# First feed-forward layer: the output unit three iterations behind its h tile, and the rests' pass last over all four chunks

## The chip, the cores and the metric

One Trainium2 chip, one core. The metric is device time in microseconds (us) of one execution of the whole program, as the median of several runs. A core has five engines with a queue each: TensorE (PE; its weight loads are shown apart as PEld), VectorE (DVE), ScalarE (ACT), GpSimd (POOL), and SyncE (SP), which here only issues DMAs. PE writes into PSUM, eight banks of 128 partitions by 2 KiB; DVE and ACT read PSUM and SBUF, POOL SBUF alone.

## The reference

Three parts in a row, in fp32:

```python
# attention over a packed set of 32 queries, 8 batches, 8 heads, 576 tokens, head size 64
p_packed = sm_attn(p, k, v)
x = sm_attn(q, p_packed, p_packed)      # then laid out as 4608 tokens x 512
# first layer: 512 -> 2048 -> 512
h = x @ w_in
g = np.maximum(h, 0.0) + alpha * np.minimum(h, 0.0)
x = g @ w_out
# second layer: 512 -> 1536 -> 512
g = x @ w_gate
x = (g / (1 + exp(-g)) * (x @ w_val)) @ w_out
```

The weights of both layers arrive as fp64 words, which the kernel turns into fp32 on the chip.

## The kernel before

An fp32 product is made of three passes of a faster matmul type (fp32r). Each operand is split into a rounded part (`hi`) and the rest (`lo`), and `mm3` (L284) adds up lo weights x hi data, hi weights x hi data, and hi weights x lo data (the rests' pass). In the profile these passes are lines L287, L288 and L289.

**The first layer** is one loop of 256 iterations (`N1`), each for one half batch `j` (288 tokens) and one slice `f` of 128 of the 2048 inner features; `order` (L648) gives the pairs. For the first two batches the slices come in two halves, so that there are 8 partial sums of 8 iterations each, and then 12 sums of 16. Iteration `it` has up to two units on PE:

- `h_unit(it)` (L734): 6 matmuls of 128x288 into one of two PSUM banks tagged `h`. The attention's second product is folded into the weights (`ppw`, made by `pp_win`, L574), so the data are the attention's weights `a2`. Then g: for the first 48 iterations (`RELU`) two Relus on ACT (L753 into the single buffer `r`, L754 into `g32`) and one DVE instruction (L755); from then on two DVE instructions that read the bank (L759, L762). `g32` has two buffers.
- `split` (L767): ACT casts `g32` to `hi` (L770), POOL subtracts to get `lo` (L772). Each has `LAG1 + 1` = 3 buffers.
- `o_unit(it - LAG1)` (L775), two iterations behind: for each of four chunks `dc` of 128 output features, the three passes into the bank `acc0` to `acc3` of that chunk, 12 matmuls in all. At the end of a sum (`stop`) the four banks are copied out, by ACT (L798) and DVE (L796) in turn, or all four added by DVE to the first half's sum (L794, for the four second halves), and stored with two DMAs on SP (L799) to `x1p` or `x1d`. `load_part` reads `x1p` back, `load_x` reads `x1d` for the second layer.

**Around these units** a table of steps (`plan`, `EARLY`, `PPW`, `STEPS`) puts the attention of later batches, the `pp_win` products, and the conversion of weights (`widen`, L205: one ACT instruction, some five on DVE, one or two on POOL for each piece of 512 columns) at given iterations, ahead of the h unit or between it and the output unit. From iteration 44 on the weights of the second layer are converted, combined (`product2`, L686) and written to DRAM (`wgvd`).

**What sets the order.** Within an engine the order is not the source's word for word. The kernel is laid out by a planner (`schedule_with_timeline_sim=True`, L1072) that takes each engine's instructions by readiness, as it reckons it, and by the source's order where several are ready; it adds the waits. On the chip each engine then runs its fixed order. What the change touches: `LAG1` (L21), the call of `split` at L765, `split` itself, `o_unit`, and by `LAG1` the main loop (L1026 to L1032).

Of the kernel before, what the change touches and what calls it, by code (L numbers as in the profile page):

```python
# [9 lines left out]
F32R = mybir.dt.float32r  # L10
# [7 lines left out]
P = 128  # L18
T = 384
WP = 4  # L20
LAG1 = 2  # L21
RELU = 48


# [72 lines left out]
def f32(ap):  # L97
    return ap.bitcast(F32)
# [3 lines left out]
def tile_kernel(  # L102
# [21 lines left out]
    nc = tc.nc  # L124
# [3 lines left out]
    KC = DM // P  # L128
# [31 lines left out]
    def utile(tag, shape, name, dt=F32):  # L160
        return upool.tile(shape, dt, tag=tag, name=name, bufs=UBUFS[tag])
# [122 lines left out]
    def mm3(o, wts, xs, start, stop, **kw):  # L284
        whi, wlo = wts
        xhi, xlo = xs
        nc.tensor.matmul(o, wlo, xhi, start=start, stop=False, **kw)  # L287
        nc.tensor.matmul(o, whi, xhi, start=False, stop=False, **kw)  # L288
        return nc.tensor.matmul(o, whi, xlo, start=False, stop=stop, **kw)  # L289
# [303 lines left out]
    for f in range(NF1):  # L593
# [10 lines left out]
        c=quad(2, natural=True),  # L604
# [120 lines left out]
    gp = gp1.enter_context(tc.tile_pool(name="g1", bufs=1))  # L725
    gs, acc, part = {}, {}, {}
# [7 lines left out]
    def h_unit(it):  # L734
        j, f, _, _ = order[it]
        b, half = divmod(j, 2)
        w = ppw[b, f // WP]
        c = slice((f % WP) * P, (f % WP + 1) * P)
        tok = slice(half * HS, (half + 1) * HS)
        hp = ps.tile([P, 512], F32, tag="h", name=f"h{it}", bufs=2)[:, :HS]  # L740
        for q2 in range(NQ):
            hi, lo = a2[NQ * b + q2]
            mm3(
                hp,
                (w[:, q2, c], w[:, NQ + q2, c]),
                (hi[:, tok], lo[:, tok]),
                q2 == 0,
                q2 == NQ - 1,
            )
        g32 = gp.tile([P, HS], F32, tag="g32", name=f"g32_{it}", bufs=2)  # L750
        if it < RELU:
            r = gp.tile([P, HS], F32, tag="r", name=f"r_{it}")
            begun[it] = nc.scalar.activation(out=r, in_=hp, func=AF.Relu)  # L753
            nc.scalar.activation(out=g32, in_=hp, func=AF.Relu, scale=-1.0)  # L754
            nc.vector.scalar_tensor_tensor(  # L755
                out=g32, in0=g32, scalar=nal[:, f : f + 1], in1=r, op0=ALU.mult, op1=ALU.add
            )
        else:
            nc.vector.tensor_scalar(  # L759
                out=g32, in0=hp, scalar1=0.0, scalar2=al[:, f : f + 1], op0=ALU.min, op1=ALU.mult  # L760
            )
            nc.vector.scalar_tensor_tensor(  # L762
                out=g32, in0=hp, scalar=0.0, in1=g32, op0=ALU.max, op1=ALU.add
            )
        gs[it] = split(gp, g32, it, LAG1 + 1)  # L765

    def split(pool, x, n, bufs):  # L767

        hi = pool.tile(list(x.shape), F32R, tag="hi", name=f"hi{n}", bufs=bufs)
        nc.scalar.activation(out=hi, in_=x, func=AF.Copy)  # L770
        lo = pool.tile(list(x.shape), F32R, tag="lo", name=f"lo{n}", bufs=bufs)
        nc.gpsimd.tensor_tensor(out=lo, in0=x, in1=f32(hi), op=ALU.subtract)  # L772
        return hi, lo

    def o_unit(it):  # L775
        j, f, start, stop = order[it]
        gx = gs.pop(it)
        hi, lo = wout[f // WP]
        for dc in range(KC):
            if start:  # L780
                acc[dc] = ps.tile([P, 512], F32, tag=f"acc{dc}", name=f"acc{dc}_{it}")[:, :HS]
            c = slice(dc * P, (dc + 1) * P)
            mm3(acc[dc], (hi[:, f % WP, c], lo[:, f % WP, c]), gx, start, stop)
        if not stop:
            return
        if f != NF1 - 1:
            x1p[j] = dram.tile([P, KC, HS], F32, name=f"x1p{j}")
        dst = x1d[j] if f == NF1 - 1 else x1p[j]
        for pr in range(2):
            xs = part[j][pr] if j in part else utile("x", [P, 2, HS], f"x1s{it}_{pr}")  # L790
            for i in range(2):
                a = acc[2 * pr + i]
                if j in part:
                    nc.vector.tensor_tensor(out=xs[:, i, :], in0=a, in1=xs[:, i, :], op=ALU.add)  # L794
                elif i:
                    nc.vector.tensor_copy(out=xs[:, i, :], in_=a)  # L796
                else:
                    nc.scalar.activation(out=xs[:, i, :], in_=a, func=AF.Copy)  # L798
            nc.sync.dma_start(out=dst[:, 2 * pr : 2 * pr + 2, :], in_=xs)  # L799
# [35 lines left out]
    def split_x(s, name):  # L835

        if name == "S2":
            src = raws_of(s, "A11")
            for e in range(2):
                nc.vector.tensor_tensor(  # L840
                    out=src[e], in0=raw2[s, "S1"][e], in1=src[e], op=ALU.subtract
                )
        elif name == "S4":
            src = raws_of(s, "A12")
            for e in range(2):
                nc.vector.tensor_tensor(
                    out=src[e], in0=src[e], in1=raws_of(s, "A11")[e], op=ALU.subtract
                )
        elif name == "S3":
            src = raws_of(s, "A21")  # L850
        else:
            src = raw2[s, "S1"] if name == "S1" else raws_of(s, name)
        tag = X_TAGS[name]
        x = wpool.tile([P, 2, 2, T], F32R, tag=tag, name=f"x{name}_{s}", bufs=WBUFS[tag])
        for e in range(2):
            nc.scalar.activation(out=x[:, 0, e], in_=src[e], func=AF.Copy)
            nc.vector.tensor_tensor(out=x[:, 1, e], in0=src[e], in1=f32(x[:, 0, e]), op=ALU.subtract)
        xs2[s, name] = x
# [22 lines left out]
    for n in ("load", "A11", "S", "S2", "A22", "A12", "S4", "S3", "S1"):  # L881
        fn = dict(load=lambda: load_x(0), S=lambda: sums_x(0)).get(
            n, lambda n=n: split_x(0, n)
# [138 lines left out]
    def steps(it, late):  # L1022
        for s in plan.get((it, late), ()):
            s()

    for it in range(N1 + LAG1):  # L1026
        steps(it, 0)
        if it < N1:
            h_unit(it)
        steps(it, 1)  # L1030
        if it >= LAG1:
            o_unit(it - LAG1)  # L1032
    gp1.close()
# [43 lines left out]
```

## Time and profile before

| | us |
|---|---|
| median of 3 runs | 1752.83 (1747.44 to 1753.05) |
| the profiled execution | 1762.42 |
| its span, first to last instruction | 1760.6 |
| PE busy in the span | 1669.6 (95%) |
| DVE / ACT / POOL busy | 1019.8 / 606.4 / 797.9 |
| first layer's loop in the span | from about 45 to 886 |

The rows are from the profiled execution. A busy time is the union of an engine's instructions; matmuls are pipelined and their ends are modelled, so the distance from one start to the next tells more than a matmul's duration. A row of waits names the engine that waited, its line and what ended the wait. In a row of a group the part after the second bar is the idle time ahead of these instructions and what ended it.

### The profile page before, as it was taken

To read this page: it belongs to the slowest core of one execution; us is meant where nothing else is said; L and a number is where in the kernel's file an instruction comes from. 1 tells how busy PE (TensorE), PEld (TensorE's weight loads), DVE (VectorE), ACT (ScalarE), POOL (GpSimd) and SP (SyncE) were. 2 spreads that over 40 slices of the span, in tenths; PEclk is the share of its full clock that TensorE was granted. 3 is DMA by queue.
4 is the path that set the end of the run, shared out by engine and by line. 5 is a ranking of instruction groups with operands and counts; after the bars stand their busy time and mean duration, and the time that the engine had idled before them with its cause. 6 is when DMAs were issued, how large, how long until landed. Compare 5 with 4: busy or idle time off the path is not lost.

```text
span 1760.6 us, 27334 instructions
## 1 busy us (share of the span) xinstructions
PE 1669.6 (95%) x10048; PEld 1474.1 (84%) x10048; DVE 1019.8 (58%) x1875; ACT 606.4 (34%) x1384; POOL 797.9 (45%) x824
## 2 busy tenths in 40 slices
PE   5698899999999999999999999999999999999997
PEld 3477688888788788889989989988988998998996
DVE  7999878676867768684633353354354344335332
ACT  5765553343433344342222232232132122223121
POOL 3666756555654555533433333334334333333332
PEclk7799999999999999999999999999999999999999
DMA  9333365455445455431364464464355445445342
GB/s 237 120 96 118 117 177 162 132 144 133 120 131 138 124 160 142 127 101 38 127 233 168 153 212 168 147 218 150 147 200 182 150 176 189 166 167 181 149 168 78
DMA packets 227750, 266.04 MB, mean 151 GB/s; under 512 B 130848, under 2 KB 190240, under 8 KB 227616
## 3 DMA queue, kind: packets, MB, share of 16 engines
q1 hardware_dynamic: 227616, 264.30, 46.9%
q8 instruction: 79, 1.29, 0.3%
q14 instruction: 55, 0.45, 0.1%
HBM read 214.70 MB, written 49.55 MB: 150 GB/s over the span
## 4 chain that ended last, share of the span: by engine, by line
PE 63%; DVE 10%; POOL 8%; DMA 7%; issue 7%; ACT 4%; SPq 1%; POOLq 0%; ACTq 0%; DVEq 0%
PE acc L287 5%; PE acc L289 5%; PE o L287 5%; PE acc L288 5%; PE o L288 4%; PE o L289 4%; PE yb L289 3%; PE yb L287 3%; PE yb L288 3%; DMA wgvd<-cva 3%; PE h L287 2%; PE xb L287 2%; PE xb L288 2%; PE xb L289 2%; PE vb L288 2%
## 5 line engine op out<-in xcount | busy, mean ns | idle before, releaser
L772 POOL TENSOR_TENSOR lo<-g,hi 128x288 fp32r<-128x288 f32 x256 | 224.0, 877 | 219.8 <-ACT hi L770 181.9
L960 POOL TENSOR_TENSOR s<-s,p 128x384 f32<-128x384 f32 x72 | 75.5, 1048 | 487.6 <-ACT s L959 487.3
L770 ACT ACTIVATE hi<-g 128x288 fp32r<-128x288 f32 x256 | 112.8, 441 | 253.5 <-DVE g L762 175.9
L919 DVE TENSOR_TENSOR u<-vb,u 128x384 f32<-128x384 f32 x144 | 80.2, 557 | 187.2 <-PE vb L289 187.2
L287 PE MATMUL o<-wp,pl 128*128 128x512 f32 x432 | 171.6, 397 | 16.1 <-POOL pl L988 15.7
L289 PE MATMUL o<-wp,ph 128*128 128x512 f32 x432 | 171.9, 398 | 0.0
L288 PE MATMUL o<-wp,ph 128*128 128x512 f32 x432 | 171.6, 397 | 0.0
L287 PE MATMUL h<-a2h,ppw 128*128 128x288 f32 x512 | 159.0, 311 | 7.8 <-DVE ppw L587 4.7
L919 DVE TENSOR_TENSOR u<-yb,p 128x384 f32<-128x384 f32 x144 | 79.6, 553 | 130.5 <-PE yb L289 128.3
L988 POOL TENSOR_TENSOR pl<-s,ph 128x384 fp32r<-128x384 f32 x144 | 142.6, 1011 | 26.0 <-ACT ph L986 21.8
L289 PE MATMUL h<-a2l,ppw 128*128 128x288 f32 x512 | 152.1, 297 | 0.0
L288 PE MATMUL h<-a2h,ppw 128*128 128x288 f32 x512 | 151.8, 297 | 0.0
L759 DVE TENSOR_SCALAR g<-h,al 128x288 f32<-128x288 f32 x208 | 105.7, 508 | 77.1 <-PE h L289 62.3
L959 ACT ACTIVATE s<-p 128x384 f32<-128x384 f32 x72 | 37.8, 525 | 303.1 <-DVE p L919 303.0
L287 PEld LDWEIGHTS h<-a2h,ppw 128*128 128x128 f32 x512 | 96.8, 189 | 39.0 <-DVE g L762 10.4
L986 ACT ACTIVATE ph<-s 128x384 fp32r<-128x384 f32 x144 | 73.3, 523 | 145.8 <-DVE s L964 129.6
L943 DVE TENSOR_TENSOR s<-xb,s 128x384 f32<-128x384 f32 x72 | 40.1, 557 | 134.2 <-ACT s L942 134.2
L287 PEld LDWEIGHTS o<-wp,pl 128*128 128x128 f32 x432 | 81.7, 189 | 30.9 <-POOL pl L988 23.9
L287 PE MATMUL xb<-xA,gv 128*128 128x384 f32 x288 | 97.9, 340 | 6.7 <-DVE u L919 6.3
L289 PEld LDWEIGHTS h<-a2l,ppw 128*128 128x128 f32 x512 | 96.5, 189 | 3.8 <-issue 3.8
L287 PE MATMUL vb<-xS,gv 128*128 128x384 f32 x288 | 97.2, 338 | 1.1 <-DVE u L919 1.1
L288 PEld LDWEIGHTS h<-a2h,ppw 128*128 128x128 f32 x512 | 96.9, 189 | 1.4 <-issue 1.4
(184 smaller groups left out, 4835.2 us busy)
## 6 DMA issues: line engine op xcount, KB each, us to landing
gv<-wgvd SPq DMA_DIRECT2D x144, 896.0 KB, 5.7
wgvd<-cva SPq DMA_DIRECT2D x84, 256.0 KB, 2.6
cva<-in_moe_w_out_dram SPq DMA_DIRECT2D x28, 512.0 KB, 3.6
v<-in_v_dram SPq DMA_DIRECT2D x16, 576.0 KB, 5.7
out_dram<-os SPq DMA_DIRECT2D x12, 768.0 KB, 3.7
cva<-in_moe_w_in_dram SPq DMA_DIRECT2D x16, 512.0 KB, 3.7
kr<-in_k_dram SPq DMA_DIRECT2D x96, 72.0 KB, 2.7
qr<-in_q_dram SPq DMA_DIRECT2D x96, 72.0 KB, 2.4
```

Of the source, the lines that this page charges most:

```text
L287: nc.tensor.matmul(o, wlo, xhi, start=start, stop=False, **kw)
L288: nc.tensor.matmul(o, whi, xhi, start=False, stop=False, **kw)
L289: return nc.tensor.matmul(o, whi, xlo, start=False, stop=stop, **kw)
L759: nc.vector.tensor_scalar(out=g32, in0=hp, scalar1=0.0, scalar2=al[:, f : f + 1], op0=ALU.min, op1=ALU.mult)
L770: nc.scalar.activation(out=hi, in_=x, func=AF.Copy)
L772: nc.gpsimd.tensor_tensor(out=lo, in0=x, in1=f32(hi), op=ALU.subtract)
L919: nc.vector.tensor_tensor(out=out, in0=bank, in1=x, op=ALU.add)
L943: nc.vector.tensor_tensor(out=s1, in0=xb, in1=s1, op=ALU.mult)
L959: nc.scalar.activation(out=s2, in_=p1, func=AF.Sigmoid)
L960: nc.gpsimd.tensor_tensor(out=s2, in0=s2, in1=p1, op=ALU.mult)
L986: nc.scalar.activation(out=hi, in_=x, func=AF.Copy)
L988: nc.gpsimd.tensor_tensor(out=lo, in0=x, in1=f32(hi), op=ALU.subtract)
```

## The change

The output unit of iteration `it` now comes in the loop's iteration `it + 3`. `hi` gets a fourth buffer; `lo` keeps three, through a new argument of `split`. And `o_unit` issues its 12 matmuls in another order: for each chunk the two passes over `hi` data, four chunks in turn, and then the rests' pass for the four chunks. `start` and `stop` stay with the first and the last matmul of each chunk. The loop has one iteration more; the number of instructions on each engine is the same.

```diff
-LAG1 = 2
+LAG1 = 3
...
-        gs[it] = split(gp, g32, it, LAG1 + 1)
-
-    def split(pool, x, n, bufs):
+        gs[it] = split(gp, g32, it, LAG1 + 1, LAG1)
+
+    def split(pool, x, n, bufs, bufs_lo):
...
-        lo = pool.tile(list(x.shape), F32R, tag="lo", name=f"lo{n}", bufs=bufs)
+        lo = pool.tile(list(x.shape), F32R, tag="lo", name=f"lo{n}", bufs=bufs_lo)
...
         hi, lo = wout[f // WP]
+        ghi, glo = gx
         for dc in range(KC):
             if start:
                 acc[dc] = ps.tile([P, 512], F32, tag=f"acc{dc}", name=f"acc{dc}_{it}")[:, :HS]
             c = slice(dc * P, (dc + 1) * P)
-            mm3(acc[dc], (hi[:, f % WP, c], lo[:, f % WP, c]), gx, start, stop)
+            nc.tensor.matmul(acc[dc], lo[:, f % WP, c], ghi, start=start, stop=False)
+            nc.tensor.matmul(acc[dc], hi[:, f % WP, c], ghi, start=False, stop=False)
+        for dc in range(KC):
+            c = slice(dc * P, (dc + 1) * P)
+            nc.tensor.matmul(acc[dc], hi[:, f % WP, c], glo, start=False, stop=stop)
```

## Rows read from the trace of the kernel before

**Rows 1.** The page: busy time of each engine, and DVE in 40 slices.

```profile
PE 1669.6 (95%) x10048; PEld 1474.1 (84%) x10048; DVE 1019.8 (58%) x1875; ACT 606.4 (34%) x1384; POOL 797.9 (45%) x824
...
DVE  7999878676867768684633353354354344335332
```

**Rows 2.** Stretches: length, each engine's busy us (instructions), clock, DMA, GB/s.

```profile
core 0: us, PE busy (x) PEld busy (x) DVE busy (x) ACT busy (x) POOL busy (x), PEclk, DMA share, GB/s
45.00:130.00 85.00, 66.81 (x425) 50.01 (x421) 80.78 (x133) 61.68 (x141) 52.29 (x44) 0.88 0.38 108
130.00:205.00 75.00, 64.79 (x410) 53.10 (x409) 70.30 (x98) 38.51 (x96) 51.75 (x43) 1.00 0.35 112
205.00:400.00 195.00, 192.34 (x1363) 164.87 (x1362) 144.41 (x293) 84.06 (x209) 112.61 (x127) 1.00 0.54 149
400.00:600.00 200.00, 192.47 (x1350) 163.74 (x1350) 145.69 (x289) 77.32 (x187) 108.13 (x123) 1.00 0.49 133
600.00:886.00 286.00, 283.49 (x2062) 256.53 (x2060) 193.98 (x385) 101.21 (x244) 136.94 (x161) 1.00 0.42 120
```

**Rows 3.** Waits of PE in 205 to 890 us: total us, times, longest us.

```profile
PE acc L289 <- POOL lo L772: 1.8, 5, 0.6
PE acc L287 <- ACT hi L770: 1.8, 3, 1.1
PE h L287 <- DVE g L762: 1.4, 3, 0.8
```

**Rows 4.** By line, 205 to 890 us: busy us, mean ns, idle before.

```profile
L772 POOL TENSOR_TENSOR lo<-g,hi 128x288 fp32r<-128x288 f32 x222 | 190.6, 860 | 197.4 <-ACT hi L770 159.4 <-issue 11.7 <-PE acc L289 10.0
...
L759 DVE TENSOR_SCALAR g<-h,al 128x288 f32<-128x288 f32 x208 | 105.7, 508 | 77.1 <-PE h L289 62.3 <-POOL lo L772 12.2 <-POOL cva L694 1.6
L770 ACT ACTIVATE hi<-g 128x288 fp32r<-128x288 f32 x222 | 97.7, 441 | 213.2 <-DVE g L762 175.9 <-DVE g L755 8.9 <-DVE mx L444 5.2
L762 DVE SCALAR_TENSOR_TENSOR g<-h,g 128x288 f32<-128x288 f32 x208 | 93.3, 450 | 3.3
```

**Rows 5.** Waits of PE in 130 to 205 us.

```profile
PE acc L287 <- ACT hi L770: 6.5, 7, 1.6
...
PE acc L287 <- DVE x1s L796: 0.8, 1, 0.8
PE acc L289 <- POOL lo L772: 0.3, 1, 0.3
```

**Rows 6.** Timeline, 139.9 to 142.2 us: start, us, engine, line.

```profile
139.89 1.54 DVE L755 SCALAR_TENSOR_TENSOR g<-g,nal,r 128x288 f32<-128x288 f32 x1
...
141.46 0.44 ACT L770 ACTIVATE hi<-g 128x288 fp32r<-128x288 f32 x1 [2.34 <-DVE g L755]
...
141.96 0.40 PE L287 MATMUL acc<-hi,wo0l 128*128 128x288 f32 x1 [1.62 <-ACT hi L770]
...
142.19 0.29 PE L288 MATMUL acc<-hi,wo0h 128*128 128x288 f32 x1
```

**Rows 7.** Waits of PE in 45 to 130 us.

```profile
PE acc L287 <- ACT hi L770: 1.2, 1, 1.2
```

**Rows 8.** Timeline of PE, 155.3 to 156.2 us.

```profile
155.28 0.29 PE L288 MATMUL acc<-hi,wo1h 128*128 128x288 f32 x1
155.41 0.29 PE L287 MATMUL h<-a2h,ppw 128*128 128x288 f32 x1
155.54 0.69 PE L289 MATMUL acc<-lo,wo1h 128*128 128x288 f32 x4
```

**Rows 9.** Timeline, 709.5 to 711.3 us, at the end of one sum.

```profile
709.52 0.39 ACT L798 ACTIVATE x1s<-acc 128x288 f32<-128x288 f32 x1
...
710.21 0.29 PE L289 MATMUL acc<-lo,wo3h 128*128 128x288 f32 x1
...
710.49 0.81 DVE L796 COPY x1s<-acc 128x288 f32<-128x288 f32 x2
```

**Rows 10.** Tile acc: who waited for it (us, times).

```profile
  POOL lo L772: 10.0, 4
```

## Prediction

> **What bounds the kernel now.** I read four views in order: the page for the whole, a table of stretches to see where TensorE (PE) is short of work, PE's waits in those stretches, and single rows of the timeline. PE is busy for 1669.6 us of the span [rows 1]. The first layer lies between about 45 and 886 us, and it has two regimes [rows 2]. From 45 to 205 us PE is busy for 131.6 of 160 us while VectorE (DVE) is busy for 151.1: DVE is full, with the weight conversions, and PE starves. From 205 to 886 us PE is busy for 668.3 of 681 us at the full granted clock of 1.00, with DVE at 68% to 74%: PE is the bound. An iteration's own matmuls are 6 for h and 12 for the output; in a run they start 0.13 us apart (155.28 to 155.41, and four in 0.69 us) [rows 8], so an output unit is 1.6 us, an h unit 0.8 and an iteration 2.4, of which 256 make 610 us that the change leaves as they are. So only PE's idle time can move, and of that only what ends with the operands of the output unit: 3.6 us in 8 waits after 205 us [rows 3], 6.8 in 8 waits from 130 to 205 [rows 5], and 1.2 before that [rows 7].
>
> **The change part by part.** The profiled execution is 1762.42 us (span 1760.6), 0.55% over the median of 1752.83; I make the sum against it and carry it over by the ratio.
>
> *The lag after 205 us.* Between the end of h(k) and the start of o(k), PE has o(k-2), h(k+1), o(k-1) and h(k+2): 4.8 us of cover. With a lag of three it is 7.2. What must fit beneath it is 0.51 + 0.45 us on DVE, 0.44 on ScalarE (ACT) and 0.86 on GpSimd (POOL), 2.3 us in all [rows 4], plus what those queues hold ahead of it. The 8 waits are the times when 4.8 us was too little, by 1.1 us at the most [rows 3], so 2.4 us more covers each. A matmul after a wait costs another 0.1 us (0.40 us and a next start 0.23 us later [rows 6], against 0.13). That is 3.6 + 0.8 = 4.4 us at most and zero at least. What is late next is h(k+3), which needs the bank of h(k+1); its cover, o(k-2), h(k+2) and o(k-1), stays 4.0 us at either lag, and it already waited 3 times [rows 3]. The waits for the rests, 1.8 us, have nothing to do with that bank, while the waits for `hi`, 1.8 us, come from a late DVE and can return there. I take 1.8 + 0.9 + 0.8 = 3.5 us gained.
>
> *The lag from 45 to 205 us.* Here o(k) waits since DVE has only just made g: DVE ends L755 at 141.43 after 1.54 us, ACT casts at 141.46, PE starts at 141.96 after 1.62 us idle [rows 6]. Putting h(k+3) ahead of o(k) gives PE nothing to do: the bank that it needs is released by the two Relus of h(k+1), the first of which writes `r`, a single buffer that DVE's g(k) has to read first. The wait for `hi` becomes a wait for the bank. DVE's own work is not changed, and it has 4.7 us idle in 75 [rows 2]. Bounds: all waits go, 6.5 + 0.8 + 0.3 and 9 restarts of 0.1, 8.5 us gained [rows 5]; or PE stands one output unit further back at 205 us, 1.6 us lost. I take zero, and zero for the 1.2 us before 130 us.
>
> There is a rule that reads this stretch otherwise. The Trainium skill, Perfetto Trace Analysis, "Optimization Strategy", says that the same gap coming back on the engine that should be saturated can mean too few buffers for the next tile. By that rule the fourth `hi` buffer would earn the 8.5 us; DVE's 70.3 busy of 75 us [rows 2] speaks against it, and it is a rival below.
>
> *The order of passes.* The same 12 matmuls and 12 weight loads per unit. The trace holds the new order already, since the planner holds back rests that are late: after l, h on four chunks come the four rests together, 0.69 us, with starts 0.13 us apart [rows 8], as in any other order. Cost zero.
>
> *The end of a sum.* 20 sums end, 19 with a unit behind them. Now the banks end 0.13 us apart instead of 0.4, so the first bank is done 0.8 us later and the second 0.5 later; the next unit's chunks also begin 0.26 us apart rather than 0.4. In the stop at 710 us the last matmul starts at 710.21 and DVE's two copies run from 710.49 to 711.30 [rows 9]: DVE was busy elsewhere when its first bank ended, so they don't move. ACT's first copy goes from 709.52 to about 710.3, over by 710.7. The next unit starts after an h unit, at 711.14: covered, and the fourth bank, wanted at 711.9, has 0.6 us to spare. Where the cover is gone, the one such wait of 130 to 205 us was 0.8 us [rows 5]: from 0 to 19 x 0.8 = 15 us. The stop read here is covered, so I take one such wait, 1 us lost. The four second-half sums whose four additions all go to DVE are the likeliest.
>
> *The buffers.* `hi` has four now, `lo` stays at three at a lag of three. So POOL's lo(k+3) needs o(k)'s rests to be through, 1.6 us after h(k+3); its operand is ready after 0.51 + 0.45 + 0.44 = 1.4 us, so POOL stands about 0.2 us each time with its other work queued behind. It stood for such a buffer 4 times before, 10.0 us in all [rows 10]. Who waits for it: g(k+5) on DVE, since `g32` has two buffers (DVE stood 12.2 us for `lo` [rows 4]). lo(k+3) ends 0.86 us after o(k); h(k+5) ends 0.8 + 1.6 + 0.8 = 3.2 us after o(k), 2.3 us later. Zero, while POOL begins it within 2.3 us.
>
> *Moved past queues.* Everything that an output unit issues goes one iteration later: its copies on ACT and DVE and its two stores per sum on SP, which pass what SP has due in 2.4 us. The readers of x1p and x1d come iterations later: nothing. The drain after the last h grows from two units to three, the start lacks one: zero. The second layer is untouched.
>
> Sum: -3.5 + 1 = -2.5 us; 1762.42 - 2.5 = 1759.9, a ratio of 0.9986, times 1752.83 gives **1750.3 us**.
>
> **The rivals.** *Starvation is relieved.* The waits from 130 to 205 us go after all, since some of them are only POOL and ACT out of step and DVE has 4.7 us of slack. For it: 8 of the 17 operand waits lie there. Against it: the single `r`. -2.5 - 8.5 = -11, or 1741.8 us.
>
> *The rests' buffers throttle.* POOL, held at lo(k+3), lets its other work pile up, a 2.3 us margin is passed, DVE's g(k+5) is late, and PE waits for a bank of h. Its price is the longest such wait, 0.8 us [rows 3]. With 3.5 us gained it passes the bound of slower from 11 such iterations on; 15 of the 222 after 205 us give 12.0 - 3.5 = +8.5, or 1761.3 us. For it: POOL's 10.0 us and DVE's 12.2 us of such waits [rows 4, 10]. Against it: POOL is 48% to 58% busy [rows 2].
>
> *It does not do what it says.* The planner orders by readiness: in the trace a rests' pass stands between matmuls of an h unit [rows 8], which no line of the source asks for. If the lag only breaks ties, nothing moves: 1752.8 us.
>
> *Cycling through banks breaks the stream.* With a bank changed at 8 places in each unit rather than at 4, PE restarts once in each: 256 x 0.1 = 25.6 us [rows 6], less 2.5, or 1776 us. Against it: the run of four banks at 0.13 us [rows 8] and a clock of 1.00 throughout [rows 2]. The Trainium skill, TensorE: Matmul & The Clock Gate, "A second HAM failure mode: psum-queue depth-cycling", describes it: a kernel whose matmuls go round the banks idles briefly between groups, and its clock swings. Those rows disagree with it here.
>
> **How the numbers follow.** A measurement of this kernel can tell about 0.3%, 5.3 us, from no change. Chances: forecast 0.42, starvation relieved 0.28, throttle 0.18, does nothing 0.08, banks 0.04. The forecast's own range is 1746 to 1756 (0 to 4.4 gained, the end of sums, 1.6 lost); a tenth of it falls below 1747.6. Faster 0.28 + 0.04 = 0.32; same 0.38 + 0.08 = 0.46; slower 0.18 + 0.04 = 0.22. The range has to take in the first rival's 1741.8 and half of the second's: **1741 to 1760**. Left out: the banks and the far half of the throttle, and the far ends of the costs.
>
> **What would show it.** Right: the waits of PE on `hi` and `lo` after 205 us nearly gone, those on the bank of h (g at L762) longer by about 1 us; from 130 to 205 us the same idle time of PE, some 10 us, with DVE as full, ended by other waits; four rests in a row in nearly every unit at 0.13 us. Wrong: PE ahead by 5 us or more at 205 us (starvation); many waits of POOL for the rests' matmuls with waits of h behind them (throttle); an unchanged order on PE (nothing); starts further apart inside units (banks). It would also be wrong if the waits of attention's steps, which the change doesn't touch, were dealt anew by the planner.

## The result, and the profile after

| | kernel before | changed kernel |
|---|---|---|
| median, us | 1749.59 (1745.38 to 1753.05) | 1760.57 (1756.9 to 1762.36) |
| ratio, 95% interval | 1 | **1.0053 [1.0035, 1.0071]** |
| profiled execution, us | 1762.42 (span 1760.6) | 1759.17 (span 1757.4) |

The change makes the kernel slower by 0.53%, about 9 us (the two medians lie 11 us apart; the interval of the ratio, 6 to 12 us, holds both). The forecast was 1750.3 us in 1741 to 1760: wrong in sign, and outside the range.

One thing has to be put aside before the traces are read side by side. The profiled execution of before is longer than that of after, against the verdict. I took a second profile of the unchanged kernel (experiment 1). The tables below cut both profiles of before, and that of after, some 2 to 5 us behind the first matmul of the second layer. The columns are those of [rows 2].

Before, first profile:

```profile
45.00:885.00 840.00, 798.90 (x5593) 687.26 (x5590) 634.39 (x1193) 361.89 (x873) 461.72 (x495) 0.99 0.45 128
885.00:1760.00 875.00, 843.98 (x4317) 771.23 (x4315) 353.56 (x612) 218.23 (x455) 319.47 (x296) 0.99 0.47 169
```

Before, second profile:

```profile
45.00:885.00 840.00, 800.51 (x5597) 689.37 (x5594) 635.54 (x1194) 362.99 (x875) 462.61 (x495) 0.99 0.45 128
885.00:1750.00 865.00, 837.06 (x4313) 768.69 (x4311) 340.91 (x612) 219.19 (x455) 325.04 (x296) 1.00 0.47 171
```

After:

```profile
45.00:891.00 846.00, 800.59 (x5592) 690.50 (x5589) 638.53 (x1195) 360.98 (x873) 463.51 (x495) 0.99 0.45 127
891.00:1757.00 866.00, 838.12 (x4320) 769.46 (x4318) 341.12 (x612) 219.62 (x455) 325.19 (x296) 1.00 0.47 171
```

From the second layer's first matmul to the end the first profile of before took 879.7 us, the second 869.3 and every other run 864 to 873; that excess belongs to that one execution. The first layer is the same in both: the second layer's first matmul starts at 880.9 and 880.4 us. In the changed kernel it starts at 888.9. So **all of the loss, 8 us, is in the first layer**. Cut exactly there, the second profile of before and that of after read:

```profile
45.00:880.40 835.40, 795.91 (x5565) 684.77 (x5562) 635.26 (x1193) 362.37 (x873) 461.81 (x494) 0.99 0.45 127
45.00:888.90 843.90, 798.49 (x5579) 688.40 (x5576) 638.53 (x1195) 360.98 (x873) 463.51 (x495) 0.98 0.45 127
```

Of the 8.5 us between these two, PE stands for 5.9 (45.4 against 39.5 us) and is busy for 2.6 more.

The granted clock of TensorE is a rival that the expectations don't name. In the changed kernel it is 0.50, the lower of its levels of 1.2 and 2.4 GHz, from 196.6 to 200.0 us, behind 10 us in which PE stood for 2.4. Matmuls that started 0.13 us apart then start 0.24 apart, and four rests take 1.16 us where they take 0.69 at the full clock:

```profile
196.99 0.44 PE L784 MATMUL acc<-hi,wo1l 128*128 128x288 f32 x1
197.22 0.44 PE L785 MATMUL acc<-hi,wo1h 128*128 128x288 f32 x1
...
197.94 1.16 PE L788 MATMUL acc<-lo,wo1h 128*128 128x288 f32 x4
```

Neither profile of before has such a stretch between 100 us and the second layer; every other kernel below has at least one. Averaged over whole executions the granted clock is 0.987 for before and 0.984 for the changed kernel; taken as span times the missing share, 6 us more are lost. Yet this explains little of the 9 us. In this profile the stretch lies where DVE is full, and by 205 us PE has done about as many matmuls as before (829 since 45 us, before 835 and 827). And among executions of the same kernel (205, of 18 kernels) 1 us more of lost clock goes with 0.19 us more of time (95%: 0.09 to 0.29): about 1 us of the 9, an estimate. No run holds the clock fixed.

The page of after, as in [rows 1]:

```profile
PE 1665.5 (95%) x10048; PEld 1476.1 (84%) x10048; DVE 1010.9 (58%) x1875; ACT 606.8 (35%) x1384; POOL 805.4 (46%) x824
...
DVE  6999978686777768675543353353354336335332
```

The stretches of after, as in [rows 2]:

```profile
45.00:130.00 85.00, 67.49 (x414) 50.43 (x411) 80.44 (x134) 60.07 (x138) 50.51 (x42) 0.87 0.33 101
130.00:205.00 75.00, 64.21 (x415) 54.79 (x414) 70.29 (x97) 41.01 (x101) 54.92 (x45) 0.98 0.42 121
205.00:400.00 195.00, 183.98 (x1305) 157.01 (x1304) 148.17 (x284) 81.01 (x203) 108.83 (x123) 1.00 0.55 148
400.00:600.00 200.00, 198.57 (x1411) 171.80 (x1409) 150.12 (x300) 77.95 (x193) 116.61 (x134) 1.00 0.50 136
600.00:886.00 286.00, 281.33 (x2021) 251.48 (x2020) 188.69 (x381) 100.48 (x241) 131.84 (x154) 1.00 0.39 111
```

Up to 205 us PE is as busy as it was (131.7 us of 160, before 131.6). From 205 to 400 us it loses 8.4 us (192.34 to 183.98), from 400 to 600 it gains 6.1 back, and from 600 to 886 it loses 2.2. These stretches are cut by time and not by work, so they don't add up to the 8 us; but the loss has no single place, it comes and goes.

PE's waits in after, 205 to 890 us, as in [rows 3] (engine, line, what ended the wait: total us, times, longest us):

```profile
PE h L287 <- DVE g L762: 7.1, 9, 1.9
PE ppt L506 <- ACT ppbd L500: 2.8, 3, 1.3
PE ppt L506 <- DVE x1p L799: 2.1, 1, 2.1
PE et L473 <- ACT E L448: 1.4, 2, 0.7
PE pp L489 <- DVE ppw L587: 1.2, 2, 1.0
PE acc L784 <- DVE x1p L799: 0.9, 1, 0.9
PE pp L489 <- DVE s2t L521: 0.8, 1, 0.8
PE acc L784 <- ACT x1s L803: 0.5, 1, 0.5
```

The waits for `hi` and `lo`, 3.6 us before, are gone. In their place stand 7.1 us for the bank of h, and 4.9 us of attention's `ppt`, 0.6 before, 2.1 of it ended by a copy of a sum; attention's `et` and `pp` wait as long as they did (3.4 us, before 3.5). In sum PE waited 16.8 us here, against 12.0 and 10.4 in the two profiles of before.

PE's waits in after, 130 to 205 us, as in [rows 5]:

```profile
PE h L287 <- ACT g L754: 4.4, 4, 2.1
PE acc L784 <- ACT hi L770: 2.8, 3, 1.4
PE acc L784 <- DVE x1s L801: 2.7, 2, 2.1
```

Two rows by line, 205 to 890 us, as in [rows 4]:

```profile
L772 POOL TENSOR_TENSOR lo<-g,hi 128x288 fp32r<-128x288 f32 x222 | 189.9, 858 | 215.8 <-ACT hi L770 133.8 <-PE acc L788 36.2 <-issue 21.4
...
L759 DVE TENSOR_SCALAR g<-h,al 128x288 f32<-128x288 f32 x208 | 105.1, 507 | 83.4 <-PE h L289 74.3 <-POOL lo L772 8.0 <-POOL cva L694 0.6
```

POOL is held by the rests' matmuls for 36.2 us, before 10.0 (12.2 in the second profile); but DVE waits for `lo` no longer than before: 8.0 us, where the two profiles of before have 12.2 and 6.6.

A unit of after in the timeline, columns as in [rows 6]: the last chunk's two passes over `hi`, the four rests in one row, the next h unit.

```profile
216.65 0.30 PE L784 MATMUL acc<-hi,wo3l 128*128 128x288 f32 x1
216.78 0.29 PE L785 MATMUL acc<-hi,wo3h 128*128 128x288 f32 x1
216.91 0.69 PE L788 MATMUL acc<-lo,wo3h 128*128 128x288 f32 x4
217.44 0.29 PE L287 MATMUL h<-a2h,ppw 128*128 128x288 f32 x1
```

### The profile page after: what moved, and what is told of

The parts are those of the page before. It is cut to its first block, busy times and chain, and to the rows that moved or that the text cites. A ratio compares the mean times of both kernels' runs of the same rounds, so it can differ in the third digit from the quotient of the medians.

```text
span 1757.4 us, 27301 instructions
## 1 busy us (share of the span) xinstructions
PE 1665.5 (95%) x10048; PEld 1476.1 (84%) x10048; DVE 1010.9 (58%) x1875; ACT 606.8 (35%) x1384; POOL 805.4 (46%) x824
## 4 chain that ended last, share of the span: by engine, by line
PE 67%; DVE 12%; DMA 6%; issue 5%; POOL 4%; ACT 4%; SPq 1%; DVEq 0%; ACTq 0%; POOLq 0%
PE o L287 5%; PE o L288 5%; PE o L289 5%; PE acc L784 5%; PE acc L785 5%; PE acc L788 5%; PE yb L287 4%; PE yb L288 4%; PE yb L289 4%; PE xb L287 3%; PE xb L288 3%; PE xb L289 3%; PE h L287 3%; PE vb L288 2%; PE vb L289 2%
## 5 line engine op out<-in xcount | busy, mean ns | idle before, releaser
L971 POOL TENSOR_TENSOR s<-s,u 128x384 f32<-128x384 f32 x72 | 101.2, 1406 | 5.6
```

The lines of the kernel that those rows point to most:

```text
L971: nc.gpsimd.tensor_tensor(out=s2, in0=s2, in1=u3, op=ALU.mult)
```

## The experiments

Four theories stood at the start. *Throttle*: three `lo` buffers at a lag of three hold up POOL. *The lag itself*: with h ahead of the output unit, waits for operands turn into waits for the bank of h. *Ends of sums*: the four banks now end 0.13 us apart, and the copies are late. *Layout*: none of these; the planner orders all engines anew whenever the source changes, and the new order is worse in places that have nothing to do with the change. For each run the start of the second layer ("x") says how much of a difference lies in the first.

### 1. The unchanged kernel once more

> The kernel before, unchanged, for a second profile of it. All theories: ratio 1.000 within 0.002. Its first profile took 1762.4 us where the median is 1751: if the second layer is 869 us long here, as in the five other kernels, and not 880, that profile's excess was its own; if it is 880 again, the order of the second layer differs from the others and the first layer of the kernel before must be some 10 us shorter than its profile showed.

Measured: 0.9996 [0.9981, 1.001], x 880.4. The comparison is good to 0.2% either way, and the tables above show what the first profile had too much.

### 2. Each half of the change alone

The lag with the old order of passes, and the new order with the old lag:

```diff
 # lag alone, against the changed kernel
-            nc.tensor.matmul(acc[dc], lo[:, f % WP, c], ghi, start=start, stop=False)
...
+            mm3(acc[dc], (hi[:, f % WP, c], lo[:, f % WP, c]), gx, start, stop)
```

```diff
 # order alone, against the changed kernel
-LAG1 = 3
+LAG1 = 2
...
-        gs[it] = split(gp, g32, it, LAG1 + 1, LAG1)
+        gs[it] = split(gp, g32, it, LAG1 + 1, LAG1 + 1)
```

> The lag of three with four hi and three lo buffers, but the passes in the order of the kernel before (lo weights, hi weights, rests, chunk by chunk). Throttle by the rests' buffers: as the changed kernel, 9 us over the kernel before (ratio 1.005), and POOL's waits for the rests' matmuls near the 36.2 us in 14 that the changed kernel shows (10.0 in 4 before). The lag itself (h ahead of o turns waits for operands into waits for the bank of h): also 1.005, but with POOL's waits free to be anything. Ends of sums (the four banks end together): no loss, 0.998 to 1.002. Planner dealing anew: any of these.

> The new order of passes at the lag of two, with three hi and three lo buffers as before. Throttle: no loss, 0.998 to 1.002, POOL's waits for the rests' matmuls near 10 us. The lag itself: no loss. Ends of sums: 5 to 9 us slower (1.003 to 1.005), with waits of PE for the copies of the banks of 5 us and more (1.7 in the kernel before, 6.3 in the changed one).

Measured: lag alone 1.0042 [1.0027, 1.0056], x 883.9; order alone 1.0067 [1.0052, 1.0083], x 895.0. PE's waits from 205 to 890 us, lag alone:

```profile
PE h L287 <- DVE g L762: 4.3, 7, 1.1
PE et L473 <- ACT E L448: 2.8, 2, 2.3
```

Order alone:

```profile
PE et L473 <- ACT E L448: 5.8, 3, 2.8
PE h L287 <- DVE g L762: 3.7, 8, 0.8
PE acc L784 <- ACT hi L770: 2.2, 3, 1.0
```

Each half costs about as much as both together, so they don't add up as two causes would. The order alone, which has neither the lag nor the short `lo`, costs most, and its longest waits are those of attention's `et`. So neither the throttle nor the lag itself is needed for such a loss.

### 3. The rests' buffers: four, and two

Four `lo` buffers (the room comes from three rows of the softmax's sums that share one, so this edit isn't the buffer alone), and two:

```diff
-        gs[it] = split(gp, g32, it, LAG1 + 1, LAG1)
+        gs[it] = split(gp, g32, it, LAG1 + 1, LAG1 + 1)
...
-                st["sx"] = sm.tile([P, 3, NB32], F32, tag="sx", name=f"sx_{g}", bufs=2)
+                st["sx"] = sm.tile([P, 1, NB32], F32, tag="sx", name=f"sx_{g}", bufs=2)
```

```diff
-        gs[it] = split(gp, g32, it, LAG1 + 1, LAG1)
+        gs[it] = split(gp, g32, it, LAG1 + 1, LAG1 - 1)
```

> The changed kernel with a fourth lo buffer; to make room, the softmax's three small rows share one (same arithmetic). Throttle: POOL's waits for the rests' matmuls fall from 36.2 us to 10 or less, the waits of PE on the bank of h from 7.1 us to 2 or less, and the time comes back to 0.997 to 1.000 of the kernel before. The lag itself: 1.005 stays, PE's waits on the bank of h stay near 7 us. Ends of sums: 1.005 stays, the waits for copies stay near 6 us.

> The changed kernel with two lo buffers instead of three: the suspected hold made harder. Throttle: POOL waits for the rests' matmuls in most iterations, and the time goes to 1.010 or more. The lag itself, and ends of sums: 1.005, not told from the changed kernel.

Measured: four 1.0051 [1.0034, 1.0068], two 1.0058 [1.0045, 1.0072], the change itself 1.0053. Waits of POOL and PE, 45 to 890 us, with four:

```profile
POOL lo L772 <- PE acc L788: 8.9, 5, 4.5
...
PE h L287 <- DVE g L762: 7.9, 8, 2.8
```

With two:

```profile
POOL lo L772 <- PE acc L788: 125.7, 76, 4.4
...
PE h L287 <- DVE g L762: 3.2, 4, 1.4
```

This settles the throttle. POOL's hold goes from 8.9 to 36.2 to 125.7 us as the buffers go from four to two, and the time doesn't follow. At two buffers even DVE waits 45.4 us for `lo`; but PE's waits for the bank of h, which were to be the consequence, are fewest there, 3.2 us.

### 4. The old order in the units that end a sum

```diff
+        if stop:
+            for dc in range(KC):
...
+                mm3(acc[dc], (hi[:, f % WP, c], lo[:, f % WP, c]), gx, start, stop)
+        else:
...
```

> The changed kernel, but the 20 units that end a sum issue their passes chunk by chunk, so that the banks end 0.4 us apart again. Ends of sums: the waits for the copies fall from 6.3 us to 2 or less and the time goes to 1.001 or less. Planner dealing anew: 1.003 to 1.007 whatever these waits do.

Measured: 1.0056 [1.0037, 1.0075]. PE's waits for copies, 45 to 890 us (the expectation's 6.3 us counts in the 2.1 us of `ppt`, which are left out from here on):

```profile
PE acc L791 <- DVE x1s L808: 6.5, 5, 2.5
```

All such waits together are 7.1 us here and 4.1 us in the changed kernel; before they were 1.7 us. Giving the banks their old spacing at the ends doesn't bring the time back, nor lessen these waits: they don't come from the 0.13 us.

### 5. Edits of the kernel before that hold nothing of the change

If it is the layout, an edit that merely alters the order of the source should cost something of the same size. Five such edits of the kernel before: a fourth `hi` buffer at the old lag; the chunks of the output unit in the order 3, 2, 1, 0; in the order 1, 2, 3, 0; the two halves of the h unit's sum the other way round; the first two passes swapped.

```diff
 # a fourth hi buffer
-        gs[it] = split(gp, g32, it, LAG1 + 1)
+        gs[it] = split(gp, g32, it, LAG1 + 2, LAG1 + 1)
 # chunks reversed (in e15: (1, 2, 3, 0))
-        for dc in range(KC):
+        for dc in reversed(range(KC)):
 # halves of h
-        for q2 in range(NQ):
+        for q2 in reversed(range(NQ)):
 # passes swapped
+            nc.tensor.matmul(acc[dc], hi[:, f % WP, c], ghi, start=start, stop=False)
+            nc.tensor.matmul(acc[dc], lo[:, f % WP, c], ghi, start=False, stop=False)
```

> The kernel before with a fourth hi buffer alone, at the lag of two and with the passes as they were. A buffer more takes no freedom away: by its own effect 0.996 to 1.000. Planner dealing anew: 1.003 to 1.007, as the other kernels, with the same places of loss.

> The kernel before with the four chunks of the output unit in reverse order: the same lag, the same buffers, the same passes, nothing that any engine needs changed. Planner dealing anew (every engine's order is laid out afresh whenever the source's order moves, and the steps were placed for the order that the kernel before had): slower by 0.3 to 0.7%, 1.003 to 1.007, with the loss at the same places as in the four other kernels (work of PE from 160 to 320 us). A cause in the lag, in the passes or in the ends of sums: 0.998 to 1.002.

> The kernel before with its chunks in the order 1, 2, 3, 0. Planner dealing anew: 1.000 to 1.007, a fifth draw for the kernel before beside 1.0003, 1.0027, 1.0035 and 1.0061. A kernel before that is no low draw: below 1.002.

> The kernel before with the two halves of the h unit's sum in the other order, which nothing else depends on. Planner dealing anew, and the kernel before fitted to its own order: 1.002 to 1.007, as with the reversed chunks. If the kernel before is no lucky draw: 0.998 to 1.002.

> The kernel before with the first two passes of the output unit changed about (hi weights, then lo weights, then the rests), the same operands at the same time. Planner dealing anew: 1.002 to 1.007. If the kernel before is no lucky draw: 0.998 to 1.002.

| edit of the kernel before | ratio, 95% | x, us | waits of PE for copies, 45 to 895 us |
|---|---|---|---|
| none (second profile) | 0.9996 [0.9981, 1.001] | 880.4 | 2.0 |
| fourth `hi` buffer | 1.0003 [0.999, 1.0015] | 880.4 | 3.3 |
| passes swapped | 1.0027 [1.0014, 1.004] | 883.3 | 6.7 |
| chunks 3, 2, 1, 0 | 1.0035 [1.0023, 1.0047] | 884.4 | 2.5 |
| chunks 1, 2, 3, 0 | 1.0043 [1.0031, 1.0055] | 885.4 | 7.6 |
| halves of h | 1.0061 [1.0041, 1.0082] | 887.9 | 2.9 |

The four edits with the same matmuls in a permuted order cost 0.27% to 0.61%, and "x" follows, with about two thirds of the loss. The change's 0.53% is one of this family. The fourth `hi` buffer costs nothing, against the 1.003 or more that its expectation had for a new layout. The dearest, two halves of a sum exchanged on PE alone, moved at least 107 of DVE's 1875 instructions, none of which the edit names (the fewest that must move to turn one trace's order into the other's; between the two profiles of before it is none). The start, from the two traces, with the rows that left their place marked by a minus and where they went by a plus:

```
 L587 TENSOR_TENSOR ppw<-ppw,ppw 128x512
-L521 STREAM_TRANSPOSE s2t<-s 128x288
 L224 SCALAR_TENSOR_TENSOR cvb<-cva,cvb 128x512
 L213 TENSOR_SCALAR cvb<-cvb 128x512
-L525 TENSOR_REDUCE sx<-s2t 128x9
 L232 TENSOR_SCALAR cva<-cvb 128x512
 L216 TENSOR_SCALAR cvb<-cvb 128x512
+L521 STREAM_TRANSPOSE s2t<-s 128x288
+L224 SCALAR_TENSOR_TENSOR cvb<-cva,cvb 128x512
+L525 TENSOR_REDUCE sx<-s2t 128x9
```

A step of the softmax (L521) now stands behind four instructions of the weight conversion that it stood ahead of, in the stretch where DVE is full. How many rows move is no measure of the cost: the fourth `hi` buffer moved at least 281 and cost nothing. Nor is each of these edits quite free of a price of its own: the rotated chunks and the swapped passes raise PE's waits for copies by 5 us, and with the halves of h exchanged the first h matmul starts 2.3 us later (53.1 against 50.8). The reversed chunks show neither, and cost 0.35%.

### 6. The same edits on the changed kernel

A pair with the same edit on both sides measures the change with the layout drawn anew each time. The diffs are those of 5, on both loops over the chunks.

```diff
-        for dc in range(KC):
+        for dc in reversed(range(KC)):
...
-        for dc in range(KC):
+        for dc in reversed(range(KC)):
```

> The changed kernel with the four chunks in reverse order in both of its loops; its partner without the change is the reversed kernel before (1.0035). Planner dealing anew (the change has no effect of its own, its 0.5% is one draw): anything from 0.998 to 1.007, over or under its partner. An effect of the change itself of about 0.4%: 1.007 or more, that is 0.3% or more over its partner.

> The changed kernel with the two halves of the h unit's sum in the other order; its partner is the run before this one. Planner dealing anew: between 0.998 and 1.007, no fixed distance to its partner. An effect of the change itself: 0.3% or more over its partner, again.

> The changed kernel with its first two passes changed about; its partner without the change was at 1.0027. Planner dealing anew: between 0.998 and 1.007, no fixed distance. An effect of the change of its own of 0.3% or more: 1.006 or more.

> The changed kernel with its chunks in the order 1, 2, 3, 0 in both loops; partner: the run before this one. Planner dealing anew: between 0.998 and 1.007, over or under its partner. An effect of the change of its own: 0.3% or more over its partner.

| edit | without the change | with it | difference |
|---|---|---|---|
| none | 1 | 1.0053 [1.0035, 1.0071] | +0.53% |
| chunks 3, 2, 1, 0 | 1.0035 | 1.0022 [1.0008, 1.0036] | -0.13% |
| halves of h | 1.0061 | 1.0057 [1.0037, 1.0077] | -0.04% |
| passes swapped | 1.0027 | 1.0063 [1.0046, 1.0081] | +0.36% |
| chunks 1, 2, 3, 0 | 1.0043 | 1.0033 [1.0022, 1.0044] | -0.10% |

The mean of the five is +0.12% with a spread of 0.30%, which makes 0.12 ± 0.37% (95%, five values). Without the first pair it is +0.02%. In three of the five the changed kernel comes out lower; the swapped passes, like the change without an edit, come out as an effect of its own would (1.006 or more was the mark). An effect of the change itself isn't shown; one of up to a few tenths of a per cent, either way, is not excluded.

### 7. A planner without its estimate of time

Both kernels, laid out with the planner's timeline estimate off, an order that the steps were not placed for:

```diff
-    with _tile.TileContext(nc, schedule_with_timeline_sim=True) as tc:
+    with _tile.TileContext(nc, schedule_with_timeline_sim=False) as tc:
```

> The kernel before laid out by the planner without its timeline estimate (the option off): a layout that the steps were not placed for. If the low time of the kernel before lies in the fit of its steps to its own layout: 1.003 or more. If not: 0.998 to 1.002.

> The changed kernel laid out in the same way, without the timeline estimate; partner: the run before this one. Planner dealing anew: within 0.4% of its partner on either side. An effect of the change of its own: 0.3% or more over it. Pairs so far: +0.5, -0.1, 0.0, +0.4 and -0.1%.

Measured: 1.0411 [1.0395, 1.0427] and 1.0427 [1.0413, 1.0442], a difference of +0.16%. The first layer of before in this layout, as in the first tables:

```profile
45.00:960.00 915.00, 828.30 (x5570) 706.59 (x5571) 634.34 (x1193) 363.73 (x872) 459.95 (x495) 0.96 0.42 117
960.00:1828.00 868.00, 838.52 (x4344) 773.92 (x4343) 347.95 (x612) 218.03 (x456) 324.38 (x297) 1.00 0.47 172
```

The same instructions with the same busy time of DVE (634.3 us) take 4% longer in another order, all of it in the first layer: the second now starts at 963.0 us instead of 880.4. PE is also busy longer, 828.3 us against 800.5, at a granted clock of 0.96 against 0.99: such an order costs waits and clock together. The order alone is worth that much, and the change again next to nothing.

## Why the prediction was wrong, point by point

- **What can move: the step that failed.** "So only PE's idle time can move, and of that only what ends with the operands of the output unit." That takes the order of every other engine as given, and PE's busy time too. The text itself says that a planner orders by readiness, and names a new deal of attention's waits in its last sentence, but it has no term, no bound and no chance for it. The runs put one there: five neutral edits draw 0.0 to 0.6%, 0 to 11 us, above a kernel before that is the lowest, with its `hi` variant, of all the layouts measured. Their mean, 0.34% or 6 us, is larger than the whole sum of -2.5 us, and none lies on the other side of zero: with that term the forecast would have been a loss of 3.4 us, and a range that took in the largest draw, 11 us, would have held the result. Why the kernel before lies so low isn't shown; that its hand-made table of steps was fitted to just this order would be an explanation. Experiment 7 came out as that expects (1.0411, where 1.003 or more was the mark), but a planner without its estimate may lay out worse whatever the table is.
- **The lag after 205 us.** The mechanism was right: waits for `hi` and `lo` fall from 3.6 us to 0 in the changed kernel, and to 0.6 us or less in every kernel with a lag of three. But the gain of 3.5 us wasn't seen in the time. Nor is it elsewhere: the fourth `hi` buffer alone lowers all of PE's waits in this stretch from 10.4 to 7.0 us and gives 1.0003.
- **The bank of h**, forecast longer by about 1 us: 1.4 to 7.1 us, a term mis-sized by 4.7 us. It isn't a fixed price of the lag either. With the halves of h exchanged the changed kernel waits 1.0 us there, and costs 1.0057 all the same.
- **The lag from 45 to 205 us**, forecast at zero: right. From 130 us on PE is busy for 64.2 of 75 us (64.8 before), DVE for 70.29 (70.30), and about the same idle time is ended by the Relus' bank (4.4 us), `hi` (2.8) and copies (2.7) where it was `hi` (6.5). The wait was turned from one thing to another, as the text said. The Trainium skill, Perfetto Trace Analysis, "Optimization Strategy", says that a gap that keeps coming back can mean too few buffers for the next tile. The trace doesn't bear that out for `hi`: with a fourth buffer alone (1.0003) the h unit of iteration 36 starts at 205.5 us, without it at 205.4 in the second profile.
- **The order of passes**, forecast at zero: right as far as PE's own pace goes. Rests stand four in a row, 0.69 us at the full clock, in 195 of the 256 units. (In the first profile of before they do in 70, so the text's "the trace holds the new order already" goes for a quarter of the units.) From 205 to 890 us, PE's next start follows that of an output matmul by 140 ns on average in both kernels (2666 in 373.9 us, 2661 in 371.7). The granted clock is 1.00 from 205 us on, and its mean over the executions is 0.983 for the lag alone, with the old order, and 0.984 for the order alone: it doesn't go by the order of passes. So the rule cited for a clock that swings when matmuls go round the banks (TensorE: Matmul & The Clock Gate, of the Trainium skill, "A second HAM failure mode: psum-queue depth-cycling") isn't borne out here. The text's "clock of 1.00 throughout" holds from 130 us on; ahead of that [rows 2] has 0.88.
- **The end of a sum**, forecast +1 us within 0 to 15: PE's waits for copies rose from 1.7 us (2) to 4.1 us (4), 1.4 us more than forecast. That the sign is right is luck: with the old spacing of the banks at the ends (experiment 4) these waits are 7.1 us, and neutral edits of before have up to 7.6.
- **The `lo` buffers**, forecast at zero: right in cost, wrong in size. I had POOL stand about 0.2 us each time; it stood 36.2 us in 14 places, up to 6.2 us at once, and at two buffers 125.7 us. At three buffers the hold doesn't reach DVE, whose waits for `lo` are 8.0 us after, 12.2 and 6.6 before; at two it does (45.4 us), and PE's waits for the bank of h are fewer still (3.2 us against 7.1).
- **The rivals.** Starvation was not relieved, the banks cost nothing, and the order did change. The throttle's 1761.3 us is within a microsecond of the measured median, by chance: its mechanism fell in experiment 3.
- **The time of before.** The excess of that profile lay in the second layer, which the change leaves alone, and the ratio was not harmed by it.

What stays open: which moved instruction costs which microsecond, and how much of a layout's cost is waiting and how much the granted clock. PE's loss grows and shrinks along the first layer (8.4 us lost, 6.1 regained, 2.2 lost), and no single wait carries it.

## What to carry to other kernels

Where a planner makes the order, an edit is two changes, the one that was meant and a new draw of everything around it; price the draw with two or three edits of no substance (a loop reversed, a buffer more), and put its spread into the range on the side on which it falls. To learn what the change itself does, put the same neutral edits on both kernels and compare the pairs. A wait that disappears, or a hold that grows, is no time by itself: here 3.6 us of PE's waits went and POOL's hold ran from 9 to 126 us, and the time followed neither.

## What had not been expected

One execution of the same program spent 353.6 us on the 612 VectorE instructions of the second layer where another spent 340.9, and took 879.7 us for that layer instead of 869.3, after a first layer of the same length (880.9 and 880.4). A single profile of a kernel can thus be 10 us off in a stretch that no edit touched, more than the effect under study; the cause isn't shown.
